# Starting one batch's last DFT two slots later and spreading it over 16 slots, into the first tile that reads it

## The chip, the cores and the metric

The kernel runs on one core of a Trainium2 chip. The metric is device time in microseconds of one execution, as a median over executions; all times below are of runs with a mean granted TensorE clock of 0.996 or more, except where a lower one is named. A profile's span is about 2 us shorter than the time of the same execution (846.2 against 848.22 us); it runs from the first to the last recorded instruction.

## The reference

Two layers in a row. The first mixes a sequence in the frequency domain, the second is a two-layer feed-forward network.

```python
X = np.fft.rfft(x, axis=1)                 # x: 8 x 3008 x 256
Yr = Xr @ w_r - Xi @ w_i + b_r
Yi = Xr @ w_i + Xi @ w_r + b_i
# soft threshold of both by 0.01
y = np.fft.irfft(Yr + 1j * Yi, n=3008, axis=1)
h = np.maximum(y.reshape(24064, 256) @ w_in, 0)    # w_in: 256 x 2048
out = (s * h * h + b) @ w_out                       # w_out: 2048 x 256
```

## The kernel before

The Fourier transforms are matmuls too: 3008 = 94 x 32, so each is a DFT over 94 points, one over 32, and back. For batch 1, which this change is about, the stages are: a forward DFT over 94 (L570, run early), the middle stages (L606 forward, L621 and L635 mixing with the weights, L665 inverse), a store of the result v to DRAM and its reload in another order as vs, and the last DFT (L718), which gives yt. The feed-forward tiles then read yt (L769, first layer) and run the second layer (L840).

TensorE's program is cut into slots. A slot is one pair of L769 matmuls of the current tile and four L840 matmuls of the tile before it, and everything else is a list of units planned into slots. There are 16 slots to a tile. Batch 0 has six tiles, so batch 1's first tile begins at slot 96, which is `mark[1]`.

```python
plan = {}

def schedule(start, span, units):
    for i, u in enumerate(units):
        plan.setdefault(start + (i * span) // len(units), []).append(u)
...
schedule(24, 42, s23_units(1))                  # middle stages of batch 1
schedule(mark[1] - 14, 12, s4_units(1))         # last DFT of batch 1: the line that changes
for b in range(2, B):
    ...
    schedule(s0 + 40, p - 48, s1_units(b))      # L570
    schedule(s1 + 2, p - 30, s23_units(b))      # L606 and on: slot 98 for batch 2
    schedule(s2 - 14, 12, s4_units(b))
```

The last DFT has 14 units, here called groups: seven ranges of n2 (0-4, 5-9, ... 25-29, 30-31) by two halves of the channels. Each takes one PSUM bank, then a copy by ScalarE or VectorE out of it.

```python
def unit(g):
    n2, w, ec = groups[g]
    ...
    ps = one_bank()                              # psf: a pool of two banks
    for j in range(w):                           # w = 5, or 2 in the last range
        h, k = divmod(n2 + j, HW)
        nc.tensor.matmul(ps[:, j * 96 : (j + 1) * 96],
                         vs[(b, h)][:, k, ec * P : (ec + 1) * P], C_t, start=True, stop=True)
    evac(yt[:, ec, n2 : n2 + w, :], ..., w * 96)
```

`evac` gives the copy to whichever of the two engines has the smaller running estimate of load. The pool psf is shared by all small stages (L570, L606, L621, L635, L665, L718). The first three tiles of batch 1 read n2 from 0 to 15, the next three from 16 to 31. The reload comes in two halves of 768 KB, n2 0 to 15 first.

## Time and profile before

The time before is 848.44 us (848.11 to 849.39, three runs).

| what the profile shows | before |
|---|---|
| span | 846.2 us |
| TensorE busy | 833.9 us, 99% |
| VectorE, ScalarE busy | 691.8 us (82%), 642.7 us (76%) |
| TensorE busy in 130 to 138 us | 7.25 of 8.00 us |
| TensorE idle in front of the first L718 of batch 1 | 0.76 us |

How to read it: TensorE has almost no idle time, so another engine's work costs nothing unless TensorE waits for it. The one wait that the tables show in the neighbourhood of the change is in the fourth and fifth row. The lines themselves are shown in the prediction. A matmul's recorded end is modelled, so costs are best read from the start of one group to the start of the next.

### The profile page before, as it was taken

The numbers are of one execution on the slowest core, as the hardware profiler recorded it, in microseconds if no ns is written. First come the engines' busy times: TensorE is split into PE (matmuls) and PEld (weight loads), VectorE is DVE, ScalarE is ACT, GpSimd is POOL, SyncE is SP. The second block draws the span as 40 slices with busy tenths as digits, with TensorE's granted clock in tenths as the row PEclk, the third lists the DMA queues.
The fourth block names the chain that finished last, engine by engine and source line by source line (L and its number), as shares of the span: only waits on it lengthen the run. The fifth ranks groups of instructions, "written<-read, shape, count | busy, mean of one in ns | idle before, by whom it ended". The sixth has DMA issues, their size and how long they took to land.

```text
span 846.2 us, 17115 instructions
## 1 busy us (share of the span) xinstructions
PE 833.9 (99%) x6653; PEld 599.6 (71%) x6653; DVE 691.8 (82%) x1026; ACT 642.7 (76%) x864; POOL 46.0 (5%) x71
## 2 busy tenths in 40 slices
PE   8999999999999999999999999999999999999997
PEld 6857766777677766777677776777667777766765
DVE  5989987888878987888888888798977888776674
ACT  5988886787778787788777887788877778666673
POOL 4341000000000001000000000000000000000000
PEclk9999999999999999999999999999999999999999
DMA  8945568224762367324761247613354223411111
GB/s 201 181 142 122 122 151 212 67 72 103 173 185 57 99 169 182 96 75 108 189 170 51 78 102 199 171 41 91 101 156 122 62 78 97 112 33 38 38 44 50
DMA packets 105747, 96.06 MB, mean 114 GB/s; under 512 B 9543, under 2 KB 97483, under 8 KB 104323
## 3 DMA queue, kind: packets, MB, share of 16 engines
q1 hardware_dynamic: 99218, 80.55, 32.9%
q0 software_dynamic: 6448, 14.42, 10.7%
q8 instruction: 52, 0.85, 0.4%
q14 instruction: 29, 0.23, 0.1%
HBM read 53.52 MB, written 46.66 MB: 118 GB/s over the span
## 4 chain that ended last, share of the span: by engine, by line
PE 89%; DVE 4%; DMA 3%; ACT 3%; issue 1%; POOL 0%; DVEq 0%; ACTq 0%; SPq 0%; POOLq 0%
PE psa L840 36%; PE psh L769 36%; PE psf L635 4%; PE psf L570 2%; PE psf L621 2%; PE psf L606 2%; PE psf L718 2%; PE psf L665 2%; ACT rt L776 1%; DVE gt L783 1%; DMA vd<-v 1%; PE psm L426 1%; DMA vs<-vd 1%; DMA x<-in_x_dram 1%; DMA F_c<-dft_fwd 0%
## 5 line engine op out<-in xcount | busy, mean ns | idle before, releaser
L776 ACT ACTIVATE rt<-psh 128x1024 f32<-128x1024 f32 (+2 forms) x384 | 386.8, 1009 | 119.6 <-PE psh L769 117.8
L783 DVE TENSOR_TENSOR gt<-rt 128x1024 f16<-128x1024 f32 (+2 forms) x321 | 383.9, 1199 | 98.3 <-ACT rt L776 97.6
L840 PE MATMUL psa<-w_out_t,gt 128*128 128x256 f16 (+1 forms) x3024 | 454.6, 272 | 0.1
L840 PEld LDWEIGHTS <-gt 128*128 128x128 f16 (+1 forms) x3024 | 301.0, 101 | 187.0 <-issue 1.4
L769 PE MATMUL psh<-yt,w_in 128*128 128x512 f16 (+1 forms) x1344 | 396.3, 378 | 0.2 <-ACT rt L776 0.2
L769 PEld LDWEIGHTS <-w_in 128*128 128x128 f16 x1536 | 142.9, 98 | 28.0 <-issue 2.0
L850 DVE SCALAR_TENSOR_TENSOR ost<-psa,s_bc,bias_bc 128x512 f32<-128x512 f32 (+2 forms) x97 | 71.0, 732 | 8.3 <-PE psa L840 6.7
L780 ACT ACTIVATE gt<-rt 128x1024 f16<-128x1024 f32 (+2 forms) x63 | 66.2, 1050 | 1.0
L640 DVE TENSOR_TENSOR ring<-psf,s 128x512 f16<-128x512 f32 x84 | 57.4, 684 | 3.7 <-PE psf L635 3.1
L170 ACT CAST v<-psf 128x512 f16<-128x512 f32 x78 | 45.3, 582 | 18.7 <-PE psf L665 18.7
L170 ACT CAST xf<-psf 128x512 f16<-128x512 f32 x82 | 47.9, 585 | 10.9 <-PE psf L606 10.8
L769 PE MATMUL psh<-tail,w_in 128*128 128x512 f16 (+1 forms) x192 | 52.1, 353 | 0.0
L170 ACT CAST u<-psf 96x512 f16<-96x512 f32 x75 | 43.4, 580 | 10.9 <-PE psf L570 10.7
L635 PE MATMUL psf<-W_g,xf 128*128 128x256 f16 x336 | 50.4, 272 | 0.0
L170 ACT CAST yt<-psf 128x480 f16<-128x480 f32 (+2 forms) x73 | 37.3, 523 | 14.2 <-PE psf L718 14.2
L213 POOL DMA_DIRECT2D x<-in_x_dram x36 | 18.7, 526 | 432.4 <-PE psf L570 431.2
L570 PE MATMUL psf<-x,A_t 94*96 94x512 f16 x103 | 39.3, 381 | 1.7 <-ACT yt L170 0.5
L646 DVE TENSOR_TENSOR ring<-ring,high 128x512 f16<-128x512 f16 x84 | 35.5, 423 | 2.3
L647 DVE TENSOR_TENSOR ring<-ring 128x512 f16<-128x512 f16 x84 | 35.4, 422 | 1.9
L645 DVE TENSOR_TENSOR ring<-ring,low 128x512 f16<-128x512 f16 x84 | 35.4, 421 | 1.6
L635 PEld LDWEIGHTS <-xf 128*128 128x128 f16 x336 | 32.9, 98 | 3.9
L718 PE MATMUL psf<-C_t,vs 96*128 96x96 f16 x448 | 33.0, 205 | 0.9 <-DMA vs<-vd 0.8
(97 smaller groups left out, 500.7 us busy)
## 6 DMA issues: line engine op xcount, KB each, us to landing
out_dram<-ost SPq DMA_DIRECT2D x152, 128.0 KB
ud<-u SPq DMA_DIRECT2D x28, 384.0 KB
us<-ud SPq DMA_DIRECT2D x28, 384.0 KB
vd<-v SPq DMA_DIRECT2D x42, 256.0 KB
vs<-vd SPq DMA_DIRECT2D x14, 768.0 KB
x<-in_x_dram POOLq DMA_DIRECT2D x28, 376.0 KB, 6.5
ring<-ring SPq DMA_DIRECT2D x280, 32.0 KB
out_dram<-ost SPq DMA_DIRECT2D x16, 120.0 KB
```

The costliest lines, as they stand in the source:

```text
L170: return None, nc.scalar.copy(out=dst, in_=src)
L570: nc.tensor.matmul(ps[0:96, :], A_t[0:N1, :], x16[(b, c)][0:N1, j * D : (j + 2) * D], start=True, stop=True,)
L635: nc.tensor.matmul(ps[:, r, :], xt[:, 2 - r, dc], W_g[:, dc, r], start=(dc == 0), stop=(dc == DC - 1),)
L640: nc.vector.tensor_tensor(out=t, in0=ps, in1=hold[i // 2][:, i % 2].unsqueeze(1).to_broadcast([P, 2, D]), op=ALU.add,)
L646: nc.vector.tensor_tensor(out=m, in0=m, in1=high, op=ALU.min)
L718: nc.tensor.matmul(ps[:, j * 96 : (j + 1) * 96], vs[(b, h)][:, k, ec * P : (ec + 1) * P], C_t, start=True, stop=True,)
L769: nc.tensor.matmul(o, w_in_t[dc][:, mc * P : (mc + 1) * P], r, start=(dc == 0), stop=(dc == DC - 1),)
L776: nc.scalar.activation(out=rt[:, :, 0:w], in_=ps[:, :, 0:w], func=AF.Relu)
L780: nc.scalar.activation(out=gt[:, :, 0:w], in_=rt[:, :, 0:w], func=AF.Square)
L783: nc.vector.tensor_tensor(out=gt[:, :, 0:w], in0=rt[:, :, 0:w], in1=rt[:, :, 0:w], op=ALU.mult)
L840: nc.tensor.matmul(ps[0:size, h, :], gts[(ti, mc // 2)][:, mc % 2, sub * size : (sub + 1) * size], w_out_t[:, mc, :], start=(mc == 0), sto ...
L850: nc.vector.scalar_tensor_tensor(out=ost[0:size, 0:k], in0=ps[0:size, 0:k], scalar=s_bc[0:size], in1=bias_bc[0:size, 0:k], op0=ALU.mult, o ...
```

## The change

Its intent: begin the last DFT of batch 1 only after its reload has landed, and give each group its own slot. The last three groups then fall in slots 96 to 98, inside the first tile that reads yt; they are n2 25 to 31, which that tile doesn't read.

```diff
-    schedule(mark[1] - 14, 12, s4_units(1))
+    schedule(mark[1] - 12, 16, s4_units(1))
```

## The prediction

> **What bounds the kernel now.** I read the page first, then the table of waits for TensorE, then the order-of-time view around the place that the change moves, then the chain that ended last.
>
> The page says that TensorE is the bound:
>
> ```profile
> PE 833.9 (99%) x6653; PEld 599.6 (71%) x6653; DVE 691.8 (82%) x1026; ACT 642.7 (76%) x864; POOL 46.0 (5%) x71
> PE 89%; DVE 4%; DMA 3%; ACT 3%; issue 1%; POOL 0%; DVEq 0%; ACTq 0%; SPq 0%; POOLq 0%
> ```
>
> The first line is the share of the span in which each engine works, the second the chain of work that ended last. No other engine comes near 99%. So an edit that only moves matmuls can win at most the gaps that it closes between them. Over the whole span, TensorE is idle 846.2 - 833.9 = 12.3 us, most of it at the two ends: the table of stretches gives 5.6 us before 48 us and 4.0 us after 750 us. Little is left for the middle.
>
> The change moves the last DFT of batch 1, the matmuls of L718 that read vs. The waits of TensorE between 118 and 150 us, where that DFT runs, are one row:
>
> ```profile
> PE psf L718 <- DMA vs<-vd: 0.8, 1, 0.8
> ```
>
> In order of time, TensorE alone, there are two places to look at (columns: start, duration, engine and line, operation, tiles, shapes, count, idle time before it and what ended it):
>
> ```profile
> 129.53 0.60 PE L840 MATMUL psa<-w_out_t,gt 128*128 128x256 f16 x4
> 130.88 0.60 PE L718 MATMUL psf<-C_t,vs 96*128 96x96 f16 x10 [0.76 <-DMA vs<-vd]
> 131.32 0.57 PE L769 MATMUL psh<-yt,w_in 128*128 128x480 f16 x2
> 131.72 0.27 PE L840 MATMUL psa<-w_out_t,gt 128*128 128x256 f16 x1
> ...
> 137.53 0.60 PE L840 MATMUL psa<-w_out_t,gt 128*128 128x256 f16 x4
> 137.96 0.88 PE L718 MATMUL psf<-C_t,vs 96*128 96x96 f16 x10
> 138.68 0.57 PE L769 MATMUL psh<-yt,w_in 128*128 128x480 f16 x2
> ```
>
> First, the DFT starts before its data: the ten matmuls of its first slot wait until 130.88. Second, the other ten-matmul slot takes 138.68 - 137.96 = 0.72 us from its start to the next group's, where the first took 131.32 - 130.88 = 0.44. What held it stands in the chain of waits, with the two transfers that the first waits for:
>
> ```profile
> 116.31 7.59 DMA vd<-v
> 124.04 6.79 DMA vs<-vd
> 130.88 0.60 PE psf L718 x10
> ...
> 137.76 0.66 DVE yt L174
> 138.47 0.37 PE psf L718 x5
> ```
>
> The store of v to DRAM and its reload take 7.59 + 6.79 us in series and decide when L718 may start. At 138.47 the second five matmuls of the doubled slot wait for a VectorE copy that frees their PSUM bank: psf has two buffers, so each group needs the bank of the group but one before it.
>
> **What the Trainium skill says.** "Perfetto Trace Analysis", section "Tensor Engine Instruction (MATMUL, LD_WEIGHTS)", says that a matmul's start is recorded and its end is estimated from its size. So I take costs from start to start, and 99% busy doesn't hide the doubled slot's loss from me: the wait table shows no row for it. "TensorE: Matmul & The Clock Gate", section "Back-to-back issue gap", gives N/2.4 + 2.5 ns for a single matmul: 109 ns for 256 columns, 42.5 ns for 96. The trace agrees: four L840 matmuls take 0.43 us from start to the next group (108 ns), and five L718 matmuls take 132.67 - 132.46 = 0.21 us (42 ns). "Perfetto Trace Analysis", section "Matmuls", advises that independent groups rotate through different PSUM banks so that copies out of one overlap matmuls into the next. The two-deep rotation here is just that, and the 0.3 us at 138 us is what a slot with two groups costs. "DMA: Bandwidth & Descriptors", section "Rules for kernel authors", advises to issue a transfer early and to wait on its semaphore late. The change does the second half: the reload still lands at about 130.9, and its reader comes later.
>
> **The change part by part.** A slot is one pair of L769 matmuls and four L840 matmuls. Batch 1's tiles begin at slot 96. Before, the 14 DFT groups go to slots 82 to 93, two of them in slots 82 and 88; from the formula in the schedule, after they go to 84-90 and 92-98, one per slot. Order of instructions in the built kernel confirms it. Nothing is added or removed on TensorE: 13,308 rows in both.
>
> Work on TensorE from the end of slot 81 (the last L840 group starts at 129.53, so its successor could start at 129.97) to the first L606 matmul of the next stage in slot 98, which starts at 147.97 before:
> - 14 slots with 480 columns: 0.41 (L769 pair) + 0.43 = 0.84 us each, 11.76 us.
> - 2 slots with 512 columns: 0.43 + 0.43, 1.72 us.
> - 12 groups of five L718 matmuls at 0.21 and two groups of two at 0.09: 2.70 us.
> - two L570 matmuls at 0.22: 0.44 us.
>
> That is 16.62 us of work in a stretch of 147.97 - 129.97 = 18.00 us; so 1.38 us are lost there. Of it, 130.88 - 129.97 = 0.91 is the wait for vs (0.76 by the table, where estimated ends are used), 0.72 - 0.42 = 0.30 is the doubled slot, and 0.17 are small bits.
>
> What it removes: slots 82 and 83 without a DFT group take 2 x 0.84 + 0.22 (an L570 that stays in slot 82) = 1.90 us, so the first L718 is reached at 129.97 + 1.90 = 131.87. The reload lands 1.0 us earlier, if it lands when it does now; nothing upstream of it has changed. So the whole 0.91 us goes. No slot holds two groups any more, so the 0.30 goes too.
>
> What it adds: the last three groups lie in slots 96, 97 and 98, in front of matmuls of the first tile that reads yt. They write n2 from 25 on, and that tile (and the two after it) reads n2 below 16, so there is no true dependency; in the built kernel's listing the L769 matmuls of slots 96 to 98 carry no wait of their own. But the next batch's first L606 group falls in slot 98 as well, right after the last DFT group, and takes the bank of the group in slot 97, which VectorE now copies, after the output's L850 and a squaring of L783 in its order. By hand: slot 95's L769 pair starts 13 slots (10.92), 11 groups (2.31) and two L570 (0.44) after 129.97, at 143.6; ScalarE's rectifier (0.97 us) runs from about 144.2 to 145.1; L850 (0.75) starts after the L840 group ends, about 144.6, and the squaring (1.16) follows to 146.5; the copy of the small group (0.36) ends at 146.9. TensorE reaches L606 at 129.97 + 16.62 = 146.6. That is a new wait of about 0.3 us, an estimate from those durations. The other copies have a slot or more to spare.
>
> Sum at the first L606: -0.91 - 0.30 + 0.3 = -0.9, and up to -0.1 of small bits, so about -0.9 to -1.0 us. TensorE is the bound from there to the end, so the shift should reach the end as it stands.
>
> Beyond that stretch only the choice of engine for the copies moves, because the running estimate of load in the program takes them in another order. The totals hardly differ: VectorE gets one squaring of 768 columns and one 192-column copy more and two copies of 480 and 512 columns fewer; ScalarE the reverse.
>
> **Rivals.** (1) A false wait: the framework could treat yt as one piece, so that each L769 of slots 96-98 waits for the copy just before it. Each would cost about a matmul group, a queue and a copy, some 1 us, so 3 us and a time near 850.5. Against it: the listing shows no such wait. (2) The gain is eaten in the crowded slot 98: if VectorE is later than by my hand count, by one more squaring (1.16), L606 waits 1.4 us and the time is as before, 848.4. VectorE is 9.52 of 12.00 us busy between 138 and 150, which leaves it some room. (3) The transfer lands later as well, because output stores now fall beside it; then part of the 0.76 comes back. The stores in that window are the same and earlier in the queue, so I give it little. (4) The new choice of engines moves small waits downstream, such as the 0.45 us before 307.22, where a VectorE copy of v held L570. That can go either way, and I allow 0.7 us for it; it is the largest part of my range.
>
> **Range and chances.** 848.44 - 1.0 = 847.44; I shade to 847.5 for the new bank wait. The three runs before spread from 848.11 to 849.39, so a median can be off by 0.4 us; with rival 4 and part of rival 2 the range is 846.3 to 848.9. Two per cent is 17 us, more than all idle time of TensorE in the span (12.3), so faster by over 2% is all but excluded; slower by over 2% would need a stall of 17 us, which no wait in the listing suggests.
>
> **What would show it.** In the changed profile: no row of L718 waiting for vs, the first L718 near 131.9, groups of five and never ten; the first L606 of slot 98 near 147.0 instead of 147.97, with a wait of some 0.3 us on a VectorE copy of yt in front of it; equal busy time of TensorE, and no wait of L769 on yt. I am wrong if L769 waits for yt copies near 145 us, if slot 98 waits over 1 us, or if the stretch gains 1 us and the rest of the kernel loses it in waits on VectorE after 150 us.

## The result

The changed kernel takes 847.57 us (846.95 to 849.42, six runs) against 848.68 us (847.46 to 850.08, six runs) for the kernel before: ratio 0.9989, 95% interval 0.9975 to 1.0002. A ratio is the mean time of one kernel's runs over that of the other's of the same rounds, so not quite the ratio of the medians. A later job of five rounds on another chip gave 847.38 against 848.21 us, 0.9990 (0.9978 to 1.0001). Each interval still touches 1; both put the gain near 0.9 us, and the profiles place it.

The page of the changed kernel has the same work on TensorE in a shorter span (845.0 us):

```profile
PE 833.8 (99%) x6653; PEld 599.6 (71%) x6653; DVE 693.6 (82%) x1026; ACT 641.8 (76%) x864; POOL 45.0 (5%) x71
PE 90%; ACT 3%; DMA 3%; DVE 2%; issue 1%; POOL 0%; SPq 0%; ACTq 0%; DVEq 0%; POOLq 0%
```

Busy time fell by 0.1 us and the span by 1.2, so it is gaps that closed. The table of TensorE's waits in 118 to 150 us, which had the one row for vs, is empty now. In order of time, TensorE alone, these are the lines that answer to those shown of before:

```profile
129.47 0.60 PE L840 MATMUL psa<-w_out_t,gt 128*128 128x256 f16 x4
129.91 0.38 PE L570 MATMUL psf<-x,A_t 94*96 94x512 f16 x1
...
131.81 0.38 PE L718 MATMUL psf<-C_t,vs 96*128 96x96 f16 x5
132.03 0.57 PE L769 MATMUL psh<-yt,w_in 128*128 128x480 f16 x2
...
146.55 0.25 PE L718 MATMUL psf<-C_t,vs 96*128 96x96 f16 x2
146.85 0.38 PE L606 MATMUL psf<-F_t,us 128*128 128x128 f16 x4
```

TensorE goes on at 129.91 with the next work, 0.44 us after its last group, and meets the first L718 at 131.81 without a wait. All groups are of five or two. The first L606 starts at 146.85 instead of 147.97, so 1.12 us of the 1.2 are won before this point. One small loss is new: two L718 matmuls take 0.09 us, so L606 could have started at 146.64. The chain of waits says what it waited for (start, duration, what):

```profile
144.72 0.74 DVE ost L850
145.46 1.06 DVE gt L783
146.53 0.28 DVE yt L174
146.81 0.04 issue
146.85 0.38 PE psf L606 x4
```

VectorE does an output, a squaring, and only then the copy that frees the bank. That is the queue that the prediction wrote out, 0.21 us of wait in place of the estimated 0.3.

### The profile page after: what moved, and what is told of

The parts are those of the page before. It is cut to its first block, busy times and chain, and to the rows that moved or that the text cites. A ratio compares the mean times of both kernels' runs of the same rounds, so it can differ in the third digit from the quotient of the medians.

```text
span 845.0 us, 17114 instructions
## 1 busy us (share of the span) xinstructions
PE 833.8 (99%) x6653; PEld 599.6 (71%) x6653; DVE 693.6 (82%) x1026; ACT 641.8 (76%) x864; POOL 45.0 (5%) x71
## 4 chain that ended last, share of the span: by engine, by line
PE 90%; ACT 3%; DMA 3%; DVE 2%; issue 1%; POOL 0%; SPq 0%; ACTq 0%; DVEq 0%; POOLq 0%
PE psa L840 37%; PE psh L769 36%; PE psf L635 4%; PE psf L570 2%; PE psf L621 2%; PE psf L606 2%; PE psf L665 2%; PE psf L718 2%; ACT rt L776 2%; PE psm L426 1%; DMA x<-in_x_dram 1%; DMA ud<-u 1%; DVE gt L783 1%; DMA us<-ud 1%; DMA F_c<-dft_fwd 0%
## 5 line engine op out<-in xcount | busy, mean ns | idle before, releaser
L840 PE MATMUL psa<-w_out_t,gt 128*128 128x256 f16 (+1 forms) x3024 | 454.4, 272 | 0.1
L840 PEld LDWEIGHTS <-gt 128*128 128x128 f16 (+1 forms) x3024 | 300.9, 101 | 187.0 <-issue 1.4
L769 PE MATMUL psh<-yt,w_in 128*128 128x512 f16 (+1 forms) x1344 | 396.3, 378 | 0.2 <-ACT rt L776 0.2
L769 PEld LDWEIGHTS <-w_in 128*128 128x128 f16 x1536 | 142.8, 98 | 27.3 <-issue 1.8
L170 ACT CAST v<-psf 128x512 f16<-128x512 f32 x78 | 45.3, 583 | 19.7 <-PE psf L665 19.7
L769 PE MATMUL psh<-tail,w_in 128*128 128x512 f16 (+1 forms) x192 | 52.1, 353 | 0.0
L570 PE MATMUL psf<-x,A_t 94*96 94x512 f16 x103 | 39.3, 382 | 1.1 <-ACT yt L170 0.5
L718 PE MATMUL psf<-C_t,vs 96*128 96x96 f16 x448 | 33.2, 205 | 0.2 <-ACT yt L170 0.2
```

Source lines behind the costliest of these rows:

```text
L170: return None, nc.scalar.copy(out=dst, in_=src)
L570: nc.tensor.matmul(ps[0:96, :], A_t[0:N1, :], x16[(b, c)][0:N1, j * D : (j + 2) * D], start=True, stop=True,)
L718: nc.tensor.matmul(ps[:, j * 96 : (j + 1) * 96], vs[(b, h)][:, k, ec * P : (ec + 1) * P], C_t, start=True, stop=True,)
L769: nc.tensor.matmul(o, w_in_t[dc][:, mc * P : (mc + 1) * P], r, start=(dc == 0), stop=(dc == DC - 1),)
L840: nc.tensor.matmul(ps[0:size, h, :], gts[(ti, mc // 2)][:, mc % 2, sub * size : (sub + 1) * size], w_out_t[:, mc, :], start=(mc == 0), sto ...
```

## The experiments

Twelve runs followed the first comparison: three of the kernels before and after once more, and nine of eight other kernels, all with correct results. For all profiles I use one measure: the stretch from the first L769 pair of slot 80 (the first with 480 columns in that place) to the first L606 of slot 98, start to start. The work in between is the same in every kernel here, except where noted. The rest is from that L606 to the end of the span. The landing is the trace's completion record of the first half of the reload. "Wait" is the idle time in front of the first L718 from start to start, as far as it was waiting for vs.

| kernel | slots | landing | first L718 | wait | first L606 | stretch | rest |
|---|---|---|---|---|---|---|---|
| before | 82-93 | 130.84 | 130.88 | 0.91 | 147.97 | 19.69 | 698.23 |
| before_again | 82-93 | 131.00 | 131.05 | 0.51 | 148.14 | 19.29 | 698.26 |
| before_third | 82-93 | 130.45 | 130.50 | 0.15 | 147.64 | 18.98 | 698.26 |
| after | 84-98 | 126.47 | 131.81 | 0 | 146.85 | 18.62 | 698.15 |
| after_again | 84-98 | 128.21 | 132.87 | 0 | 147.90 | 18.62 | 698.10 |
| shift_only | 84-95 | 130.59 | 132.31 | 0 | 147.35 | 18.63 | 698.35 |
| spread_only | 82-96 | 130.34 | 130.39 | 0.45 | 147.12 | 18.87 | 698.08 |
| end_97 | 84-97 | 127.90 | 132.71 | 0 | 147.53 | 18.41 | 698.07 |

The first L606 by itself misleads: the time at which slot 80 begins varied from 128.2 to 129.3 us among executions whose program is the same up to there, so after_again reaches L606 a microsecond later than after, at the same stretch.

**after_again**: the changed kernel, no edit, five rounds.

> The changed kernel once more, to narrow the interval and to see a second profile. All theories: the gain of about 1.1 us in the stretch up to the first L606 of slot 98 repeats (ratio to before 0.9987 to 0.9990, about 847.5 us), unless the reload of vs lands at another time in each execution: then the gain of single executions scatters between 0.3 and 1.4 us and the median stays near 1.

847.38 us (847.13 to 848.19, five runs) against 848.21 us, ratio 0.9990. The stretch repeats to the hundredth, 18.62 us. So the time at which the reload lands made no difference to it in these two profiles, where it landed at 126.47 and at 128.21 us.

**before_again and before_third**: the kernel before, no edit, one look each.

> The kernel before once more, for a second profile. If the landing of the reload of vs is the same in each execution, the wait of L718 for vs is 0.7 to 0.8 us again and L606 of slot 98 starts near 148.0. If it varies (in the profile of the changed kernel the store of v was 2 us quicker), the wait lies between 0 and 1.5 us and L606 between 147.1 and 148.8.

> The kernel before a third time. In the profiles so far the first half of the reload landed between 126.5 and 131.0 us from the start, whatever the kernel, and in both profiles of the kernel before it was late (130.8 and 131.0). If the landing is chance, this execution may fall early (126.5 to 128.7): then there is no wait for vs, the stretch from the first L769 pair of slot 80 to the first L606 is 18.8 us (18.41 of work, 0.3 of the doubled slot, 0.07 small), and even the kernel before loses only 0.4 us there. If it falls late: a wait of 0.3 to 0.8 us and 19.2 to 19.7 us.

848.39 and 847.90 us. The reload was late all three times, but TensorE's own arrival at slot 82 varied as well, and so did the wait: 0.91, 0.51 and 0.15 us. In the third profile it is too short for the table of waits, and shows only in the starts (order of time, TensorE):

```profile
129.91 0.60 PE L840 MATMUL psa<-w_out_t,gt 128*128 128x256 f16 x4
130.50 0.60 PE L718 MATMUL psf<-C_t,vs 96*128 96x96 f16 x10
```

Four L840 matmuls take 0.44 us, so TensorE was free at 130.35. The second doubled slot, though, takes 0.72 us in all three profiles (here from 137.63 to 138.35). The expectation for a late landing, 19.2 to 19.7, was missed low by before_third's 18.98.

**shift_only**: the start alone.

```diff
-    schedule(mark[1] - 14, 12, s4_units(1))
+    schedule(mark[1] - 12, 12, s4_units(1))
```

> Only the start moves by two slots (slots 84 to 95, two slots with two groups remain). Theory A, the gain is the wait for the reload of vs: that row is gone, first L718 near 131.8, first L606 near 147.1 if the second doubled slot still loses 0.3 us, near 146.8 if it doesn't, time 0.9 to 1.3 us under before (ratio about 0.9988). Rival B, the gain is from having one group per slot: the time stays within 0.3 us of before and TensorE finds another wait in place of the one on vs.

847.67 us (847.46 to 848.04), ratio 0.9991 (0.9980 to 1.0003): a gain of 0.5 us in medians and 0.8 by the ratio, less than the 0.9 to 1.3 expected, though the intervals are too wide to hold that against it. The profile decides. Here the reload landed as late as in the kernel before, 130.59, and still nobody waited for it: theory A. The doubled slots are both there:

```profile
132.31 0.59 PE L718 MATMUL psf<-C_t,vs 96*128 96x96 f16 x10
132.74 0.57 PE L769 MATMUL psh<-yt,w_in 128*128 128x480 f16 x2
...
133.58 0.38 PE L718 MATMUL psf<-C_t,vs 96*128 96x96 f16 x5
134.01 0.38 PE L570 MATMUL psf<-x,A_t 94*96 94x512 f16 x1
...
139.29 0.59 PE L718 MATMUL psf<-C_t,vs 96*128 96x96 f16 x10
139.72 0.57 PE L769 MATMUL psh<-yt,w_in 128*128 128x480 f16 x2
```

Ten matmuls in 0.43 us each time: neither doubled slot loses time within itself. What cost 0.3 us in the kernel before was that the copy of the group before the doubled slot, whose bank its second group takes, had been given to VectorE, behind a squaring of 1.16 us (it began at 136.69; the copy ran from 137.76). But the first doubled slot does cost something one slot later: L570 starts 0.43 us after a group of five that takes 0.21. The chain of waits says why:

```profile
132.07 0.97 ACT rt L776
133.04 0.92 ACT yt L170 x2
133.97 0.04 issue
134.01 0.38 PE psf L570
```

Both copies of that doubled slot fell to ScalarE, one after the other and behind a rectifier, and L570 needs the second one's bank. That is the 0.22 us by which 18.63 exceeds the 18.41 of end_97. So moving the start took away the wait for vs, and what the banks cost shrank from 0.3 to 0.2 us without the spread.

**spread_only**: the spread alone.

```diff
-    schedule(mark[1] - 14, 12, s4_units(1))
+    schedule(mark[1] - 14, 16, s4_units(1))
```

> Only the spread over 16 slots (slots 82 to 96), the start as before. Theory A: the wait for vs stays (0.8 us in the table of waits if the reload lands as it did), only the doubled slot's 0.3 us go, first L606 near 147.7, time 0.3 us under before (ratio 0.9996). Rival B: the whole gain of 1.1 us is there (ratio 0.9987).

847.35 us (847.16 to 849.74), ratio 0.9994 (0.9982 to 1.0007). The times alone cannot tell this run from shift_only; its median is even the lower one, against theory A. The table of TensorE's waits can:

```profile
PE psf L718 <- DMA vs<-vd: 0.3, 1, 0.3
```

The wait for vs is still there, 0.45 us from start to start, and it is all that is lost beyond end_97's stretch (below): 18.87 is 18.41 plus 0.46. So the spread by itself took away the whole loss at the banks, as expected.

**end_97**: the changed kernel without the shared slot 98.

```diff
-    schedule(mark[1] - 14, 12, s4_units(1))
+    schedule(mark[1] - 12, 14, s4_units(1))
```

> Start as in the change, but 14 slots (84 to 97, one group in each), so that no group shares slot 98 with the next batch's first L606 group. Theory A with the crowded slot: no wait for vs, and the 0.2 us in front of the first L606 are gone too, first L606 near 146.6, time 1.3 us under before, 0.2 under the change (ratio 0.9985). Rival: the bank wait only moves to another slot, and the time equals the change's.

847.16 us (846.92 to 847.69), ratio 0.9985 (0.9974 to 0.9997): the only one of the close variants whose interval lies below 1. The chain of waits near slot 98 is TensorE alone, each piece beginning where the one before it ends:

```profile
146.74 0.09 PE psf L718 x2
146.82 0.43 PE psh L769 x2
147.26 0.44 PE psa L840 x4
147.69 0.22 PE psf L606 x4
```

The stretch is 18.41 us, 0.21 below the change's, which is just the wait of L606 that the changed kernel showed. By hand, 16.62 us of work (the prediction's sum) and the two slots 80 and 81 (1.69 us from 128.28 to 129.97) give 18.31, so 0.1 us is all that is left to win here. In this stretch this version beats both kernels; its profiled execution as a whole does not (845.6 us, slot 80 began late, at 129.12). Its median time is 0.2 us under the change's, which the intervals don't separate.

**late_8**: later still, up to the true dependency.

```diff
-    schedule(mark[1] - 14, 12, s4_units(1))
+    schedule(mark[1] - 8, 14, s4_units(1))
```

> Later still, slots 88 to 101: the last group that the first tile of batch 1 really reads is in slot 95, right in front of it, and four groups share slots with the next stage. Theory A, that two slots were enough to pass the landing: no gain over the change; L769 of slot 96 waits up to 1 us for the copy of yt from slot 95 and L606 up to 0.5 us for banks, so 847.5 to 849 us, ratio 0.9988 to 1.0005. If later were simply better: under 847.2.

847.43 us (846.83 to 847.77), ratio 0.9990 (0.9975 to 1.0005). The stretch is 18.02, with three groups (0.21 + 0.09 + 0.09 us) now behind the first L606, so 18.41 in like terms. The waits that I had allowed for did not come, so the time is just under the range that I had given: TensorE's table for 128 to 150 us has no row. Later is neither better nor worse, as far as a gain of two tenths can be seen. In these runs one had only to be past the landing.

**early_2, early_4, early_6 and early_4_look**: the suspected cost made larger.

```diff
-    schedule(mark[1] - 14, 12, s4_units(1))
+    schedule(mark[1] - 16, 12, s4_units(1))     # early_2; -18 in early_4 and early_4_look, -20 in early_6
```

The four expectations, in the order early_2, early_4, early_6, early_4_look:

> The DFT two slots earlier than before (slots 80 to 91), halfway to the run that began four slots earlier. Theory A, each slot earlier adds its 0.87 us to the wait for vs: wait 1.5 to 2.7 us in the profile, time 1.0 to 2.2 us over before (849.2 to 850.4 us) with the granted clock at 1.0. Rival, that a stall only starts to cost past some length: as before, within 0.3 us.

> The cost under suspicion made larger: the DFT of batch 1 starts four slots earlier than before (slots 78 to 89). Theory A: TensorE then waits for vs some 3.5 us longer than before (4 slots of 0.87 us), 2 to 4.5 us in all, and the whole of it reaches the end: 850 to 852.5 us, ratio 1.002 to 1.005. Rival B, that the place of the start matters little and one group per slot makes the gain: within 0.5 us of before.

> Six slots earlier (slots 76 to 87). The wait for vs alone gives 3.5 to 5 us in the profile and 3.5 to 5 us over before (852 to 853.5 us). If a long stall also lowers the clock that TensorE is granted afterwards (two of the four runs that began four slots earlier had a mean clock of 0.994 and 0.996 and took 5.5 us longer than the fastest of them), the table of stretches shows a clock well under 1.0 in the few us after the stall and the time is 855 to 858 us, in every run.

> The kernel that begins four slots earlier once more, for a second profile. Its runs were 849.6, 851.3, 855.1 and 855.1 us. If this one falls at 855 and the clock theory holds, the wait for vs is above 3 us and the clock after it is under 1.0; if it falls at 850 to 851 the wait is 1.8 to 3 us and the clock 1.0.

| run | time, us | landing | first L718 | wait | mean clock |
|---|---|---|---|---|---|
| early_2 | 848.38 (847.83 to 849.19) | 128.38 | 129.04 | none for vs | 0.997 to 1.0 |
| early_4 | 849.59, 855.10, 855.05, 851.26 | 128.65 | 128.70 | 2.00 | 1.0, 0.996, 0.994, 1.0 |
| early_4_look | 848.32 | 127.08 | 127.12 | 0.51 | 1.0 |
| early_6 | 852.17, 858.53, 853.20, 852.11 | 126.96 | 127.00 | 2.40 | 0.996, 0.995, 0.995, 0.995 |

The profiled execution is the first of each; the landing, the first L718 and the wait are of it alone. early_2 missed its expectation: no wait for vs, and the time as before (ratio 1.0002), because the reload landed at 128.38 there, 2.1 to 2.6 us earlier than in the three profiles of the kernel before. So a rule of "0.87 us for each slot earlier" does not hold for single executions; the landing moves too much. The direction is clear only further out: early_4 has the ratio 1.0054 (1.0022 to 1.0085), early_6 1.0075 (1.0037 to 1.0112). The other expectations were met in part or missed: early_4's wait lies at the low end of its range, and only one of its four times in the range of 850 to 852.5; early_4_look fell below both of its cases (848.32 us, a wait of 0.51); early_6's wait is under its 3.5 us, three of its times are in the first range and none in the second, though the clock did fall.

Part of that is not waiting. In early_6's profile, order of time on TensorE, the stall is followed by slow matmuls:

```profile
124.16 0.60 PE L840 MATMUL psa<-w_out_t,gt 128*128 128x256 f16 x4
127.00 0.98 PE L718 MATMUL psf<-C_t,vs 96*128 96x96 f16 x10 [2.24 <-DMA vs<-vd]
127.79 1.05 PE L769 MATMUL psh<-yt,w_in 128*128 128x512 f16 x2
128.63 0.42 PE L840 MATMUL psa<-w_out_t,gt 128*128 128x256 f16 x1
```

And the table of stretches (busy us and instruction counts of each engine, then the granted clock, DMA share and GB/s) has the clock:

```profile
126.00:128.00 2.00, 1.00 (x11) 0.93 (x12) 0.00 (x0) 0.38 (x1) 0.00 (x0) 0.74 0.98 238
128.00:130.00 2.00, 2.00 (x9) 1.04 (x7) 1.79 (x2) 0.67 (x2) 0.00 (x0) 0.50 0.99 237
130.00:132.00 2.00, 2.00 (x21) 1.47 (x20) 0.66 (x1) 1.12 (x3) 0.00 (x0) 0.91 0.88 266
```

The stretch before, 122 to 126 us, has a clock of 1.00. After 2.40 us of idling TensorE was granted half its clock. The shares of 0.74 and 0.91 put this half clock at about 126.96 to 130.36 us, 3.4 us in all. The L769 pair takes 0.84 us instead of 0.43. From 127.00 to the next L718 at full speed, at 131.22, it took 4.22 us for work that takes 2.58 at full speed (two pairs 0.86, eight L840 0.86, ten and five L718 0.64, one L570 0.22), so the clock added 1.64 us to the wait. The two together, 4.04 us, are about what this execution took over the kernel before of the same rounds (852.17 against 848.26 us). early_4's profiled execution waited 2.00 us and kept its clock at 1.00. Its two executions of 855 us had a mean clock of 0.996 and 0.994, which fits the same loss; they have no trace, so what happened in them is inferred. early_6's one run of 858.53 us is not explained at all.

**source_2**: the reader stays, the producer begins earlier.

```diff
-    schedule(24, 42, s23_units(1))
+    schedule(22, 42, s23_units(1))
```

> The DFT stays where it is before (slots 82 to 93), but the stage that produces v for batch 1 begins two slots earlier (22 in place of 24). Theory A: vs lands about 1.7 us earlier, the wait for vs is gone without moving its reader, first L606 near 147.1, time 0.9 us under before (ratio 0.9989). Rival B: as before. A new wait for us at slot 22 would show as a row of L606 and would take the gain back.

848.86 us (848.61 to 849.04), ratio 1.0008 (0.9991 to 1.0025): the expected gain is not there. The first half of the reload landed at 126.43, the wait for vs is gone and the stretch is 18.72 us, between the kernel before and the change. But slot 80 begins only at 129.72, against 128.28, 128.85 and 128.66 in the three profiles of before. Upstream the wait tables (60 to 100 us, then 100 to 128 us) have rows that the first and third profile of the kernel before don't:

```profile
PE psf L621 <- DVE xf L612: 0.2, 1, 0.2
...
PE psf L665 <- DVE u L174: 0.3, 1, 0.3
PE psf L570 <- ACT v L170: 0.3, 1, 0.3
```

Together 0.8 us of the 0.9 to 1.4 by which slot 80 is late: in this profile the middle stages fell against other users of the two banks, and what was won at L718 was paid there. It is one profile, and slot 80 began as late as 129.28 us in after_again, whose program up to there is that of the kernel before; so a part of the delay may be scatter, and the cause of the lost gain is argued, not shown.

## Why the prediction was right

The time on record was 847.5 us in a range of 846.3 to 848.9; the two comparisons gave 847.57 and 847.38. The range holds the time before (848.44) too, so lying in it says little; it is the waits in the profiles that test the mechanism. That the median came within 0.1 us is in part luck, as the sum below shows. Point by point:

- *The bound.* Right: TensorE's busy time is unchanged and the gain is closed gaps. (The 13,308 rows are from a listing that is not on record; the pages count 6653 matmuls and as many weight loads in both kernels.) The rest after L606 is the same to a tenth or so in before and after (698.23 to 698.26 against 698.10 to 698.15), so a shift at slot 98 reaches the end undiminished.
- *"So the whole 0.91 us goes."* The mechanism is right; shift_only shows it with a landing as late as the kernel before's. The size was that of one execution. Three profiles of the kernel before lost 0.91, 0.51 and 0.15 us there, 0.52 on average.
- *"No slot holds two groups any more, so the 0.30 goes too."* The loss was in all three profiles of before, and it went. That 0.3 us "is what a slot with two groups costs" was too general: of shift_only's two doubled slots, one costs nothing and the other 0.22 us, one slot later. What costs is a bank whose copy stands behind other work, a squaring on VectorE in the kernel before, a rectifier and another copy on ScalarE in shift_only. The first doubled slot had such a cost too, inside the 0.17 us of "small bits": in the first profile L570 starts at 131.91, 0.08 us after it could have, when ScalarE has copied that slot's first group.
- *The new wait of about 0.3 us before L606.* There, 0.21 us, on the copy and behind the two instructions named; end_97 removes it.
- *The sum.* By the three and two profiles, the stretch shrank from 19.32 on average to 18.62: 0.70 us, with -0.52 for vs, -0.30 for the bank and +0.21 for the new wait making -0.61, and 0.09 of small bits. The predicted -0.9 to -1.0 took the largest of the three waits for the typical one; the measured times (0.8 to 1.1 us apart in medians) don't contradict either, so the close hit of the time is no proof of the sizes.
- *Rival 1, a false wait on yt.* Not seen: no row for L769 in slots 96 to 98. *Rival 2, the gain eaten in slot 98.* A fifth of it, not all. *Rival 3, a later landing.* Not seen: both profiles of after have it earlier (why, is said below). *Rival 4, other engine choices downstream.* I called it the largest part of the range and allowed 0.7 us. Over the eight profiles of the first table the rest varies by 0.28 us in all (698.07 to 698.35). That term was mis-sized; the scatter between the profiled executions comes from the landing and from what precedes slot 80. The slowest executions of either kernel (849.42, 850.08) have no trace.

What the landing depends on was not asked in these runs, but their traces show something. The reload landed at 130.3 to 131.0 us in all four profiles with the reader at slot 82 and the producer in its old place, and that late in only one (shift_only) of the nine with the reader elsewhere (126.5 to 128.7 in the rest). In those five, GpSimd had issued a load of 376 KB of the next batch's x before the reload was issued, which itself waits for the store of v to land. In the first profile of the kernel before (order of time; POOL is GpSimd, SPq the queue of SyncE):

```profile
122.22 0.51 POOL L213 DMA_DIRECT2D x<-in_x_dram  x1 [11.95 <-PE psf L570]
...
124.04 0.80 SPq L681 DMA_DIRECT2D vs<-vd  x2
```

And in that of the changed kernel, where the load of x came at 122.17, behind the reload:

```profile
121.42 0.80 SPq L681 DMA_DIRECT2D vs<-vd  x2
```

In the five profiles the reload is 0.29 to 1.82 us behind the load of x, x lands first (126.7 to 130.1 us) and the reload takes 6.8 to 7.9 us. In the other nine (source_2 is one) the reload is ahead of it, or 0.10 us behind in early_4, and lands first; it takes 5.1 to 6.2 us, in source_2 6.9. So a store of v that lands a microsecond later can put the reload behind another transfer. No run moved the load of x, so that the order is the cause is argued from fourteen profiles and not shown. Why the store's landing varies stays open, and so whether it was chance that all four profiles with the reader at slot 82 were late ones: the programs up to there are alike.

## What to carry to other kernels

When a kernel is bound by one engine and its profile has a single wait of under a microsecond, look at when the awaited transfer lands in several executions, and at which other transfers are issued just before it, and place its reader past the latest landing; here a few slots too many cost nothing (late_8), as long as the true reader is later still. When work is spread out, look whose banks it will meet in each slot, and in front of which instructions the copy out of a bank is queued. For differences of a tenth of a percent, compare the profile from one fixed instruction to another, since the times of single executions scatter more than the effect.

## What the Trainium skill lacked or had wrong

- "TensorE: Matmul & The Clock Gate", section "What's actually happening", has the clock fall back after an idle window of about 3.4 us (3413 ns). In early_6 a gap of 2.40 us was followed by a granted clock of 0.50 in 128 to 130 us and a loss of 1.64 us; a gap of 2.00 us in early_4 was not. The half clock lasted about 3.4 us, as long as the page's window, but the idling before it was shorter than one.
- The same page, section "Back-to-back issue gap", gives 81 ns per matmul of 128 columns as the sustained rate with weight loads in between. Here four L606 matmuls, each with its own weight load, take 147.07 - 146.85 = 0.22 us, 55 ns each, which is its figure for a single gap. For 512 columns it gives 131 ns; an L769 pair of 512 columns takes 0.43 us, 215 ns each, again the single gap. L718 with 96 columns takes 42 ns.
- No page gives the spread of a transfer's duration from one execution to the next: the first half of the reload, 768 KB each time, took 5.1 to 7.9 us from issue to landing (121.42 to 126.47 in after, 122.48 to 130.34 in spread_only), 6.8 or more in all five profiles where a load of 376 KB had been issued just before it.
